# Projections in pairs on 64-row tiles beside the scores, with one pool of seven PSUM banks

## The chip, the core and the metric

The kernel runs on one core of a Trainium2 chip. A core has a matrix engine (TensorE, PE in the profile, with its weight loads shown apart as PEld), a vector engine (DVE), a scalar engine (ACT), a third one for elementwise work (POOL), and a queue (SP) that issues all of this kernel's DMAs. Matmul results go to PSUM, which has eight banks of 128 x 512 floats. DVE and ACT read PSUM; POOL works on the other memory, SBUF. The metric is the device time of one execution in microseconds, lower is better.

## The reference

Two attention blocks, A and B, each over 2048 tokens of 512 features with 32 heads of 16 features. They are computed alike, but A masks its scores to a window of 256 tokens (a query sees itself and the 255 tokens that come before it), and B has no mask. The outputs stand side by side.

```python
B, S, D = x.shape                      # 1, 2048, 512
qkv = (x @ wqkv).reshape(B, S, 3, H, Dh).transpose(2, 0, 3, 1, 4)
q, k, v = qkv[0], qkv[1], qkv[2]
scores = einsum("bhqd,bhkd->bhqk", q, k) * (Dh ** -0.5)
mask = (idx[:, None] - idx[None, :] >= 0) & (idx[:, None] - idx[None, :] < 256)   # block A only
scores = where(mask, scores, -1e9)
p = softmax(scores)
out = einsum("bhqk,bhkd->bhqd", p, v).transpose(0, 2, 1, 3).reshape(B, S, D) @ wo
```

## The kernel before

Heads go in 8 groups of four, queries in 4 chunks of 512, so each block has 32 units (group, chunk). Precise products are made of faster ones: each operand is split into a rounded part and a remainder, and a product is the sum of three matmuls (part by part, part by remainder, remainder by part).

**Projections** (letter `p` in the order; `project_qk`, `project_v`, `products`, L189). One projection makes 128 x 512 results from a contraction over 512 features: 4 slices of 128 features, three matmuls each, so 12 matmuls 128 rows deep and 512 columns wide, into one bank. ACT takes the result out (L254, L331, or L250 for the first pair of heads' groups, where DVE still subtracts from the bank); q and k are split by POOL and written to DRAM, from where they are loaded in the layout that the scores need (tiles `oq` for q, `opk` for k). There are 96 such projections in the first part of the program, 48 for each block.

**Row maxima** (`m` for block A, L427, `e` and `m` for block B, L379, from `max_item` and `max2`). For 128 queries, two heads' scores are made at once: two matmuls 48 rows deep, one on rows 0 to 63 of the array and one on rows 64 to 127, into two adjacent banks. DVE reduces them to maxima (A: a masked copy L436 and a reduction L437; B: one reduction L383).

**The transpose** (`t`, `max_rows`, L505). When a unit's maxima are all there, DVE splits them in three (tile `nm`, 48 columns), PE transposes them by one matmul, ACT copies them out and two small DMAs put them as three further rows under q. So the subtraction of the maximum happens inside the score matmul.

**Scores** (`s`, `scores`, L538). Two heads, again one on each half of the array's rows, 51 rows deep, each into a bank of its own; ACT's exponential (L545) takes them out, POOL zeroes what the mask hides (L555).

**Weighing** (`w` for A at L584, L569 for B). The values are multiplied onto the exponentials of four heads at once, 17 columns each, on four tiles of 32 columns of the array.

So the array is used in four shapes: whole (projections), two tiles of 64 rows (maxima, scores), four tiles of 32 columns (weighing), and 64 columns for the transpose's 48.

The program has two parts. In the first part all of block A's attention, all 96 projections of q, k and v, and the first maxima of block B run in a fixed order, the string `ORDER_A`, one letter a step; `ORDER_P` says which projection each `p` is. The loop at the end takes one letter after the other and issues it on PE, whatever its operands' state: the engines then wait for one another by semaphores. The class `Model` keeps an estimated clock for each engine; from it the loop decides when loads and stores are issued on SP, and when work that follows (the splits on POOL and DVE) is issued, but not the order on PE. In the second part block B's scores and weighing run by another fixed pattern (`ORDER`), with the output projections in between.

In the first part the banks are three kinds: three single ones (`e`) for scores, one (`o`) in which a unit's weighing accumulates, and two pairs (`p`) for maxima. A projection or a transpose takes an `e` bank, or while no scores have begun half of a `p` pair.

## Time and profile before

| | |
|---|---|
| median of 3 runs | 1828.41 us (1828.36 to 1829.36) |
| the profiled execution's own time | 1835.78 us |
| its span | 1834.0 us, of which the first part until the first weighing of block B 558 us |
| TensorE matmuls in the profile | 14392, of which L189 1536, L538 2752, L427 512, L379 2048, L505 64 |

The page of the profile gives for each engine its busy time, and below it the chain of work that ended last. PE is drawn as busy nearly throughout, but matmuls are pipelined and their ends are modelled, so a row's length says little; the distance from one row's start to the next one's is what the work took on PE, with any wait in it. The rows of the timeline merge equal instructions: "x12" are twelve matmuls. The columns are start, length, engine, line, operation, tiles, shape and count.

### The profile page before, as it was taken

How to read it: one execution, taken by the hardware profiler on the slowest of the kernel's cores; microseconds unless marked ns; L12 is line 12 of the kernel's file. 1: busy time of each engine (PE TensorE's matmuls, PEld its weight loads, DVE VectorE, ACT ScalarE, POOL GpSimd, SP SyncE). 2: the span in 40 equal slices, each digit the busy share in tenths (PEclk: the TensorE clock that was granted, in tenths of full speed). 3: DMA queues.
4: the chain of work that ended last, by engine and by line, in shares of the span. 5: the costliest groups of instructions: out<-in, count | busy, mean ns of one | idle time of the engine just before them, and what ended most of it. 6: DMA issues, size and time to landing. Idle time of an engine off the chain costs nothing.

```text
span 1834.0 us, 37708 instructions
## 1 busy us (share of the span) xinstructions
PE 1815.2 (99%) x14392; PEld 902.5 (49%) x14392; DVE 1529.6 (83%) x2275; ACT 1404.5 (77%) x2750; POOL 648.8 (35%) x1333
## 2 busy tenths in 40 slices
PE   8999999999999999999999999999999999999999
PEld 6666656666664444444344444444444444444436
DVE  4677677766779777799999999999999999999901
ACT  4366656565548777799999999999999999999983
POOL 0367877564673333023321023430012322122320
PEclk9999999999999999999999999999999999999999
DMA  8755756545554222311210131121031121010012
GB/s 263 205 176 185 219 174 188 164 157 153 170 180 112 93 78 82 97 29 34 63 37 17 30 67 48 29 63 31 16 75 29 34 63 36 17 49 13 31 36 92
DMA packets 129158, 166.72 MB, mean 91 GB/s; under 512 B 23013, under 2 KB 58853, under 8 KB 128965
## 3 DMA queue, kind: packets, MB, share of 16 engines
q1 hardware_dynamic: 128976, 164.31, 30.4%
q8 instruction: 113, 1.85, 0.4%
q14 instruction: 69, 0.56, 0.1%
HBM read 94.49 MB, written 68.19 MB: 89 GB/s over the span
## 4 chain that ended last, share of the span: by engine, by line
PE 96%; DVE 2%; ACT 1%; DMA 0%; POOL 0%; SPq 0%; issue 0%; ACTq 0%
PE ps_all L569 29%; PE ps_all L189 20%; PE ps_all L538 20%; PE ps_all L379 19%; PE ps_all L584 4%; PE ps_all L427 3%; ACT p L545 1%; DVE mt L437 1%; PE ps_all L505 1%; DVE ps_all L436 0%; DVE mt L383 0%; DMA in<-xT_A 0%; DMA opk<-parts 0%; POOL p L555 0%; POOL x L139 0%
## 5 line engine op out<-in xcount | busy, mean ns | idle before, releaser
L545 ACT ACTIVATE p<-ps_all 128x512 f32<-128x512 f32 x2432 | 1260.8, 597 | 154.9 <-PE ps_all L538 99.9
L383 DVE TENSOR_REDUCE mt<-ps_all 128x2 f32<-128x1024 f32 x1516 | 1194.4, 867 | 72.6 <-PE ps_all L379 72.1
L538 PE MATMUL ps_all<-oq,opk 51*128 51x512 f32 (+2 forms) x2752 | 781.4, 408 | 6.0 <-ACT p L545 5.4
L379 PE MATMUL ps_all<-opk,oq 48*128 48x512 f32 x2016 | 674.3, 438 | 0.3
L569 PE MATMUL ps_all<-p,vt 128*17 128x256 f32 (+1 forms) x6056 | 587.8, 460 | 0.5 <-ACT ou L595 0.5
L538 PEld LDWEIGHTS ps_all<-oq,opk 51*128 51x128 f32 x2752 | 399.0, 185 | 193.4 <-ACT p L545 170.9
L379 PEld LDWEIGHTS ps_all<-opk,oq 48*128 48x128 f32 x2016 | 308.2, 184 | 313.8 <-DVE mt L383 176.8
L555 POOL TENSOR_SCALAR_AFFINE_SELECT p<-p 128x256 f32<-128x256 f32 x480 | 179.8, 407 | 151.6 <-ACT p L545 144.7
L569 PEld LDWEIGHTS ps_all<-p,vt 128*17 128x17 f32 x6056 | 100.7, 95 | 223.8 <-issue 213.1
L189 PE MATMUL ps_all<-x,w 128*128 128x512 f32 x768 | 201.0, 412 | 6.1 <-ACT x L138 5.9
L454 POOL TENSOR_TENSOR mu<-mt 128x16 f32<-128x16 f32 x31 | 6.8, 221 | 503.6 <-DVE mt L383 503.6
L436 DVE COPY_PREDICATED ps_all<-mone,ps_all 128x256 f32<-128x256 uint16 x224 | 94.8, 423 | 93.1 <-PE ps_all L427 92.2
L189 PEld LDWEIGHTS ps_all<-x,w 128*128 128x128 f32 x768 | 144.2, 194 | 48.0 <-ACT x L138 6.9
L437 DVE TENSOR_REDUCE mt<-ps_all 128x2 f32<-128x512 f32 x224 | 155.2, 693 | 7.7
L623 POOL TENSOR_TENSOR rd<-ld,minus 128x32 f32<-128x32 f32 x15 | 81.9, 5458 | 219.2 <-DMA ld<-od 219.2
L254 ACT ACTIVATE raw<-ps_all 128x512 f32<-128x512 f32 x56 | 33.5, 598 | 108.7 <-PE ps_all L189 106.4
L584 PE MATMUL ps_all<-p,vt 128*17 128x384 f32 (+2 forms) x1408 | 96.3, 389 | 0.0
L189 PE MATMUL ps_all<-w_v,x 128*128 128x512 f32 x384 | 95.6, 398 | 0.0
L427 PE MATMUL ps_all<-opk,oq 48*128 48x384 f32 (+2 forms) x512 | 91.5, 378 | 1.9 <-DVE mt L437 1.6
L189 PE MATMUL ps_all<-w_o,x_o 128*128 128x512 f32 x384 | 92.5, 395 | 0.0
L189 PEld LDWEIGHTS ps_all<-w_o,x_o 128*128 128x128 f32 x384 | 70.6, 188 | 29.5 <-issue 13.6
L189 PEld LDWEIGHTS ps_all<-w_v,x 128*128 128x128 f32 x384 | 70.0, 188 | 18.7 <-issue 2.7
(74 smaller groups left out, 742.4 us busy)
## 6 DMA issues: line engine op xcount, KB each, us to landing
parts<-st SPq DMA_DIRECT2D x64, 512.0 KB
oq<-parts SPq DMA_DIRECT2D x128, 128.0 KB
opk<-parts SPq DMA_DIRECT2D x128, 128.0 KB
od<-ou SPq DMA_DIRECT2D x64, 256.0 KB
vd<-vst SPq DMA_DIRECT2D x32, 272.0 KB
oq<-parts SPq DMA_DIRECT2D x128, 64.0 KB
opk<-parts SPq DMA_DIRECT2D x128, 64.0 KB
t<-od SPq DMA_DIRECT2D x32, 256.0 KB
```

Source lines behind the costliest of these rows:

```text
L189: nc.tensor.matmul(ps, l(u), r(v), start=start and k == 0, stop=stop and k == n - 1)
L379: nc.tensor.matmul(ps[:, n], q[rows, 128 * qt:128 * qt + 128], k[rows, kc * QC:kc * QC + QC], start=True, stop=True)
L383: nc.vector.tensor_reduce(out=m[:, a:a + len(heads), r, qt, kc], in_=ps, axis=AX.X, op=ALU.max)
L427: nc.tensor.matmul(two[:, a, 0:w], opq[b, g, c][rows, r, 128 * qt:128 * qt + 128], opk2(g)[rows, r, t0:t1], start=True, stop=True)
L436: nc.vector.copy_predicated(two[:, :, 256:384], later, two[:, :, 0:128])
L437: nc.vector.tensor_reduce(out=m[:, :, r, qt, 0], in_=two[:, :, 128:384], axis=AX.X, op=ALU.max)
L538: nc.tensor.matmul(ps[x][:, col:col + n1], opk2(g)[rows, pr, 128 * k:128 * k + 128], opq[b, g, c][rows, pr, q0:q0 + n1], start=True, stop= ...
L545: nc.scalar.activation(p[:, a0 + x, :w], ps[x][:, :w], AF.Exp, scale=SCALE)
L555: nc.gpsimd.affine_select(out=v, in_=v, pattern=[[0, 2], [sign, 128]], compare_op=ALU.is_ge, fill=zero_fill, base=base, channel_multiplier ...
L569: nc.tensor.matmul(o[32 * j:32 * j + VW, q0:q1], vt[(g // 2) % 2][:, kt, vc:vc + VW], pts[1, g, c, kt, j // 2][:, j % 2, q0:q1], start=kt ...
L584: nc.tensor.matmul(o[32 * j:32 * j + VW, q0:q0 + w], vt[(g // 2) % 2][:, kt, vc:vc + VW], pts[b, g, c, m, j // 2][:, j % 2, col:col + w], ...
L623: nc.gpsimd.tensor_tensor(rd, ld, minus, op=ALU.pow)
```

## The change

**Projections on half tiles.** Forty of the 96 projections run as twenty pairs, each in four steps (letter `g`, `half_rows`, L331 of the changed kernel). The contraction of 128 features of each slice is cut into rows 0 to 63 and rows 64 to 127. In the first two steps the upper half of the array works on rows 0 to 63 of the one projection into the one bank, while the lower half works on rows 64 to 127 of the other projection into another bank; in the last two steps it is the other way round, and each bank accumulates what was missing. One step is 6 times two matmuls 64 rows deep, so a pair of projections is 48 half-height matmuls in 24 twos. So that no bank is written by both halves of the array at once, PE waits before the third step, by an added dependency, for an instruction of another engine that read a result of PE from after the second step. Other letters stand between the second and the third step for that.

**One pool of banks.** The three `e` banks and the two `p` pairs become one pool `u` of seven adjacent banks (`o` moves to bank 0). Maxima take two free neighbours, all else any free ones; of several that would do, the one with the fewest free neighbours is taken.

**The transpose.** `nm` becomes two constant tiles of 2 x 32 columns with the unused columns zero; the transpose becomes two matmuls of 32 columns, which write rows 0 to 31 and 32 to 63 of the bank. The array's shape for it is then the weighing's, 32 columns.

**The order.** `ORDER_P` and `ORDER_A` are written anew: 56 letters `p`, 80 letters `g`, and the same numbers of `m`, `s`, `w`, `t` and `e` as before. The model's constants for a change of the array's shape differ by shape. The second part's order on PE is the same but for the second matmul of each transpose; one projection stands behind the first part's last weighing.

How the order moves on PE. Before, in the late part of block A, a projection of 12 matmuls (L189, operands `x` of the tokens and `w` of the weights) stands between scores (L538) and maxima (L379, L427):

```order
L538 MATMUL ps_all<-oq_6_3_4867,opk_73 128x384 x2
L538 MATMUL ps_all<-oq_6_3_4867,opk_73 128x128 x2
L189 MATMUL ps_all<-w_v_3436,x_2_0_2762 128x512 x3
L189 MATMUL ps_all<-w_v_3620,x_2_1_2848 128x512 x3
L189 MATMUL ps_all<-w_v_3636,x_2_2_2914 128x512 x3
L189 MATMUL ps_all<-w_v_3666,x_2_3_2987 128x512 x3
L379 MATMUL ps_all<-vt_75,qe 128x512 x2
L427 MATMUL ps_all<-opk_74,oq_7_2_5454 128x384 x2
L538 MATMUL ps_all<-oq_7_0_5070,opk_74 128x384 x2
L538 MATMUL ps_all<-oq_7_0_5070,opk_74 128x128 x2
```

Each `p` of this kind goes from tiles of 64 rows to the whole array and back. After, in the same stretch, this is the end of one first step, the work between it and the second step, and the second step's beginning (L331 takes turns between the two projections of a pair, L491 are maxima of A, L603 scores):

```order
L331 MATMUL ps_all<-x_3_1_3382,w_2_0_4288 128x512
L331 MATMUL ps_all<-w_v_3652,x_0_1_2037 128x512
L491 MATMUL ps_all<-opk_76,oq_7_1_5545 128x384 x2
L603 MATMUL ps_all<-oq_6_3_5106,opk_75 128x384 x2
L603 MATMUL ps_all<-oq_6_3_5106,opk_75 128x128 x2
L331 MATMUL ps_all<-x_3_2_3407,w_2_0_4288 128x512
L331 MATMUL ps_all<-w_v_3772,x_0_2_2091 128x512
```

All of it is in one shape, tiles of 64 rows. In the whole first part the array's shape changes 393 times before and 265 times after, and the runs in the whole array are 86 before and 46 after, counted in the two orders.

The transposes stood in a shape of their own between two others, here behind the weighing (L584) and ahead of scores:

```order
L584 MATMUL ps_all<-p_6_3_1_0_5562,vt_76 17x256 x2
L584 MATMUL ps_all<-p_6_3_1_1_5599,vt_76 17x256 x2
L505 LDWEIGHTS nm_7_1_5571
L505 MATMUL ps_all<-ident,nm_7_1_5571 48x128
L538 MATMUL ps_all<-oq_7_0_5070,opk_74 128x384 x2
```

After, they are two matmuls each, next to the weighing in its shape (L649 is the weighing, L570 the transpose):

```order
L491 MATMUL ps_all<-opk_75,oq_4_3_3592 128x384 x2
L570 LDWEIGHTS nm_74
L570 MATMUL ps_all<-ident,nm_74 32x128
L570 LDWEIGHTS nm_74
L570 MATMUL ps_all<-ident,nm_74 32x128
L649 MATMUL ps_all<-p_3_3_2_0_3576,vt_78 17x384 x2
L649 MATMUL ps_all<-p_3_3_2_1_3586,vt_78 17x384 x2
```

The diff, cut to its core:

```diff
+CHUNK = 6
 ORDER_P = (
-    "Aq00 Aq01 Ak00 Av13 Av00 Av03 Aq02 Av20 Ak01 Av10 Av21 Ak02 Av02 Av33 Aq03 Av01 Ak03 Av12 Av11 Aq13 Aq10 "
+    "Aq00 Ak00 Av11 Av10 Aq01 Av03 Ak01 Ak02 Av01 Av13 Aq02 Av12 Av02 Aq03 Av00 Ak03 Av23 Ak11 Av20 Ak10 Av21 "
...
 ORDER_A = (
-    "ppppppppppmmpmmpmmpmmpmmpmmtppmmpmmspsmmptpmsmswsmmpmsmwsmptmmspmswmsmpsmwsmmpmswsmmpmsmwtsmmswsmpmm"
+    "pppppppppmmpmmppmmggmmpmmgtmgmmpmmgsgmspmsgmsgmstwmmmppmsgsmgmmpmsgmmgmtwwmmspmsgsmgmswsgmsgmwtssmws"
...
-        self.mode, self.turn = "f", 170
-        self.banks = {"e": [0] * 3, "p": [0] * 2, "o": [0]}
+        self.mode, self.turn = "f", dict(f=210, h=200, c=139)
+        self.banks = {"u": [0] * 7, "o": [0]}
...
+    def take2(self):
+        self.t["PE"] = max(self.t["PE"], self.pair())
+        free = self.free()
+        n = min((free[i] + free[i + 3], i) for i in range(6) if free[i + 1] and free[i + 2])[1]
+        self.banks["u"][n:n + 2] = [self.NEVER] * 2
+        return n
...
+    nmt = [cst.tile([128, 2, 32], BF16, name=f"nm{i}") for i in range(2)]
...
+    def half_rows(stage, pairs, banks):
+
+        turn, q0 = divmod(CHUNK * stage, 12)
+        for q in range(q0, q0 + CHUNK):
+            k, i = divmod(q, 3)
+            u, v = ((0, 0), (0, 1), (1, 0))[i]
+            for a in range(2):
+                l, r = pairs[a ^ turn][k]
+                rows = slice(64 * a, 64 * a + 64)
+                op = nc.tensor.matmul(view(banks[a ^ turn]), l(u)[rows], r(v)[rows], start=turn == q == 0,
+                                      stop=turn == 1 and q == 11)
+                if turn and q == a == 0:
+                    tc.add_manual_dep(op.ins, min(since)[2].ins.name, LANDED, reason="the row tiles change banks")
+        M.pe("h", CHUNK * 233)
...
-        nc.tensor.transpose(ps[:48, :128], nm.rearrange("p a s j q -> p (a s j q)"), ident)
-        nt = sb.tile([48, 128], F32, name=f"ntr_{n}", tag="ntr")
-        nc.scalar.activation(nt, ps[:48, :128], AF.Copy)
+        for a in range(2):
+            nc.tensor.transpose(ps[32 * a:32 * a + 32, :128], nm[:, a], ident)
+        nt = sb.tile([64, 128], F32, name=f"ntr_{n}", tag="ntr")
+        op = nc.scalar.activation(nt, ps[:64, :128], AF.Copy)
...
-        banks = [M.take("e") for _ in range(heads)]
+        banks = [M.take("e" if b else "u") for _ in range(heads)]
...
+        elif x == "g":
+            if stage == 0:
+                two = its_a[nb:nb + 2]
+                nb += 2
+                banks = [M.take("u") for _ in range(2)]
+            half_rows(stage, [(pairs_qk if f == project_qk else pairs_v)(*a) for f, *a in two], banks)
+            stage += 1
+            if CHUNK * stage == 12:
+                since.clear()
+            elif CHUNK * stage == 24:
+                stage = 0
+                for (f, *a), bank_ in zip(two, banks):
+                    (end_qk if f == project_qk else end_v)(*a, bank_, view(bank_))
+                    made.add((f, *a))
```

`since` collects, from the end of the second step on, each evacuation or reduction that ACT or DVE is given, with the model's time for it; the dependency goes to the one that is done first. `end_qk` and `end_v` are the second halves of `project_qk` and `project_v`, split off unchanged.

More of the change, by code (lines that the diff above doesn't have):

```diff
@@ L201, in view, with take2, release2 @@
         pool, n = bank
-        first, width = {"e": (0, 1), "o": (3, 1), "p": (4, 2), "s": (6, 1)}[pool]
-        n = first + width * n + (pool == "e" and n > 2)
+        if pool == "u":
+            return ps_all[:, n + 1]
+        first, width = {"e": (1, 1), "o": (0, 1), "p": (4, 2), "s": (6, 1)}[pool]
+        n = first + width * n
         return ps_all[:, n] if width == 1 else ps_all[:, n:n + 2]
+    def take2():
+        n = M.take2()
+        return [("u", n), ("u", n + 1)], ps_all[:, n + 1:n + 3]
+    def release2(banks, t):
+        for b in banks:
+            M.release(b, t)
     ident = cst.tile([128, 128], BF16, name="ident")
@@ L422, in max_item @@
         w = t1 - t0
-        bank = M.take("p")
-        two = view(bank)
+        banks, two = take2()
         for a in range(2):
@@ L929, in load_next @@
         f(*a)
+    stage, two, banks = 0, None, None
     todo_a = list(ORDER_A)
```

138 lines of the change are left out of this document (81 added, 57 removed), and 6 rows, old and new, of the table ORDER_P.

## The prediction

> **What bounds the kernel now.** I read the page first: its engines, then its chain of work.
>
> ```profile
> PE 1815.2 (99%) x14392; PEld 902.5 (49%) x14392; DVE 1529.6 (83%) x2275; ACT 1404.5 (77%) x2750; POOL 648.8 (35%) x1333
> ...
> PE 96%; DVE 2%; ACT 1%; DMA 0%; POOL 0%; SPq 0%; issue 0%; ACTq 0%
> ```
>
> The chain runs on PE for 96% of the span, so what PE needs for an instruction is what counts. The change touches the first part, so next come the sums by stretch, the first part and the rest (columns: length, then busy time of PE, PEld, DVE, ACT, POOL, the granted clock, the DMA engines' share, GB/s), and two stretches of 7 us in it:
>
> ```profile
> 5.00:558.00 553.00, 543.91 (x3924) 357.73 (x3924) 379.93 (x798) 309.50 (x612) 328.70 (x630) 0.99 0.60 187
> 558.00:1834.00 1276.00, 1271.25 (x10470) 544.78 (x10469) 1148.49 (x1476) 1093.04 (x2137) 316.64 (x688) 1.00 0.18 49
> 262.00:269.00 7.00, 6.97 (x20) 4.98 (x20) 3.41 (x12) 2.25 (x5) 2.42 (x7) 0.52 0.59 200
> 276.00:283.00 7.00, 7.00 (x31) 4.97 (x24) 4.71 (x10) 3.34 (x7) 5.17 (x10) 0.52 0.36 121
> ```
>
> In the first part DVE is busy for 69%, ACT 56%, POOL 59%: PE is ahead of them all, and none would stop it from being some per cent shorter. In two stretches the granted clock was 0.52; they cost this execution 2 x 7 x 0.48 = 6.7 us. It took 1835.78 us where the median is 1828.41, 7.4 us less, so I suppose that the timed runs are without them. The terms below are differences on PE, worked out from rows at full clock, and I take them off the median.
>
> What does PE lose in a change of the array's shape? The timeline of PE, a projection (L189) between scores and maxima on 64-row tiles, twice:
>
> ```profile
> 472.07 0.50 PE L538 MATMUL ps_all<-oq,opk 51*128 51x384 f32 x4
> 472.50 3.02 PE L189 MATMUL ps_all<-w_v,x 128*128 128x512 f32 x12
> 475.45 0.50 PE L379 MATMUL ps_all<-vt,qe 48*128 48x512 f32 x2
> 475.78 0.34 PE L427 MATMUL ps_all<-opk,oq 48*128 48x384 f32 x2
> 475.96 0.40 PE L538 MATMUL ps_all<-oq,opk 51*128 51x384 f32 x4
> 476.28 3.02 PE L189 MATMUL ps_all<-x,w 128*128 128x512 f32 x12
> 479.23 0.44 PE L427 MATMUL ps_all<-opk,oq 48*128 48x384 f32 x2
> 479.51 0.40 PE L538 MATMUL ps_all<-oq,opk 51*128 51x384 f32 x4
> 479.75 0.39 PE L427 MATMUL ps_all<-opk,oq 48*128 48x384 f32 x2
> ```
>
> and, from the start of the program, projections that follow each other:
>
> ```profile
> 26.42 2.88 PE L189 MATMUL ps_all<-x,w 128*128 128x512 f32 x12
> 29.14 2.88 PE L189 MATMUL ps_all<-w_v,x 128*128 128x512 f32 x12
> 31.86 2.88 PE L189 MATMUL ps_all<-x,w 128*128 128x512 f32 x12
> ```
>
> Starts count, not lengths. Among its like a projection takes 2.72 us (227 ns a matmul); alone 2.95 (472.50 to 475.45), 0.23 more. Ahead of it, the scores of a 384 and a 128 wide two take 0.24 where the next is in the same shape (479.51 to 479.75), 0.32 where a projection follows (475.96 to 476.28): 0.08 more. And the first two in the shape after it take 0.28 at a width of 384 (479.23 to 479.51) where the second takes 0.18 (475.78 to 475.96): 0.10 more. So one projection alone costs 0.40 us beyond its work: two changes of shape at some 0.09 each, and in either shape a first instruction whose successor comes 0.10 late.
>
> **The change part by part.** *What half-height twos cost.* Block B's scores and maxima are twos of the same width, 512, on the two halves, with 51 and 48 rows instead of 64:
>
> ```profile
> 901.25 0.50 PE L538 MATMUL ps_all<-oq,opk 51*128 51x512 f32 x1
> 901.25 0.73 PE L379 MATMUL ps_all<-opk,oq 48*128 48x512 f32 x2
> 901.59 0.62 PE L538 MATMUL ps_all<-oq,opk 51*128 51x512 f32 x2
> 901.82 0.40 PE L379 MATMUL ps_all<-opk,oq 48*128 48x512 f32 x1
> 902.20 1.05 PE L569 MATMUL ps_all<-p,vt 128*17 128x512 f32 x8
> ...
> L379 PEld LDWEIGHTS ps_all<-opk,oq 48*128 48x128 f32 x2016 | 308.2, 184 | 313.8 <-DVE mt L383 176.8 <-issue 131.5 <-ACT p L545 3.0
> ```
>
> Three twos: the second begins 0.34 us after the first (the late second once more), the third 0.23 after the second. In the timeline's starts over all of block B the second interval is 0.228 to 0.238. These twos wait for banks, those of a projection stand in sixes with nothing to wait for; I take 0.232, and 0.228 and 0.238 as ends. 480 twos take the place of 480 whole matmuls at 0.227: +2.4 us, +0.5 to +5.3.
>
> The Trainium skill, TensorE: Matmul & The Clock Gate, section The mechanism, has a rule that speaks against this: a weight load overlaps with running matmuls only where the row group differs. Here each half's next weights go to the half that is at work. By that rule loads and matmuls would take turns; the time is among the rivals. The trace does not agree: 0.23 us from the second two to the third has no room for a load of 0.18 behind a matmul.
>
> *Shapes saved by projections.* There are 40 runs in the whole array fewer, and all but one of the 79 runs of `g` stand between maxima or scores. 40 x 0.40 = -16.0 us. To the edges of these rows, 0.38 to 0.42, it is -15.2 to -16.8.
>
> *Shapes saved by transposes.* What one costs now:
>
> ```profile
> 394.25 0.45 PE L538 MATMUL ps_all<-oq,opk 51*128 51x128 f32 x4
> 394.54 0.34 PE L427 MATMUL ps_all<-opk,oq 48*128 48x384 f32 x2
> 394.81 1.06 PE L584 MATMUL ps_all<-p,vt 128*17 128x256 f32 x16
> 395.79 0.24 PE L505 MATMUL ps_all<-ident,nm 128*48 128x128 bf16 x1
> 395.96 0.55 PE L538 MATMUL ps_all<-oq,opk 51*128 51x128 f32 x4
> ...
> 368.20 0.62 PE L584 MATMUL ps_all<-p,vt 128*17 128x256 f32 x8
> 368.75 0.44 PE L427 MATMUL ps_all<-opk,oq 48*128 48x384 f32 x2
> ```
>
> 16 weighing matmuls ahead of a transpose take 0.98 us, 8 ahead of maxima 0.55, so 8 alone 0.43 and the change 0.12, the same in front of a transpose as of anything. The transpose takes 0.17 with the change behind it, so some 0.06 itself. Of the 128 changes of shape that go in the first part, 80 are the projections'; the other 48 at 0.10 are -4.8 us, and 11 further late seconds on 64-row tiles at 0.10 are -1.1. The second matmul of 33 transposes costs 0.06 each, +2.0 us (no row has a second one: it could be nothing, or 0.17 as a lone one, 0 to +5.6). In block B 31 transposes stand behind a weighing: 31 x (0.06 - 0.11) = -1.6 (-3.4 to +1.9). Together -5.5, between -9.3 and +1.6.
>
> *Steps entered.* A 384 wide two that follows a short one takes 0.23 instead of 0.18 (394.25 to 394.54 is 0.29 for 0.06 + 0.23), its successor's weights being late. 45 of the 79 runs of `g` come behind a 384 wide two: at most 45 x 0.05 = +2.2, or 0 where it would have been so anyway.
>
> *Waits.* These are waits in the first part (in all, times, longest), the first one of the weight loads:
>
> ```profile
> PEld ps_all L538 <- ACT p L545: 28.6, 63, 0.9
> ...
> PE ps_all L538 <- ACT p L545: 5.2, 13, 0.7
> ...
> PE ps_all L427 <- DVE mt L437: 1.6, 6, 0.6
> ...
> PE ps_all L538 <- DMA oq<-ntr: 0.3, 1, 0.3
> ```
>
> Most come from scores whose bank ACT hasn't emptied. I walked both orders with the prices above and looked, at each wait of PE for ACT or DVE in the first part, how far back stands the matmul which that engine reads. Nearer than 1.0 us are 69 before, and these lose 17 us in the trace, all the others 7. After, 62 are nearer. So I expect the same losses, though a pair keeps two of seven banks for 6.5 to 13 us. The new wait ahead of the third step has 1.9 us or more of other work in front of it in all 20 pairs, and in two alone PE still names it, 1.3 and 1.4 us behind: nothing. What is queued behind it would be the third step and the maxima after it, and DVE and ACT would run dry. What is lost where the same work of the others stands in a part that is 3% shorter I put at +2 us, with 0 and +20 as ends: from none of the waits to one more microsecond in each pair.
>
> ACT, DVE and SP have the same instructions (a copy of 64 partitions for one of 48 has the same width); POOL has one memset more at the start. The first pair of projections waits for the second weights instead of the second tokens, while the third then waits less: nothing.
>
> The sum: 2.4 - 16.0 - 5.5 + 2.2 + 2 = -14.9 us; 1828.4 - 14.9 = **1813.5 us**.
>
> **The rivals.** *Banks run out* (slower). With five banks left for maxima in neighbours and for scores, PE stands before L491 and L603 in the middle of each pair. The sum without waits is -16.9, so from 0.85 us a pair on the gain is gone; at 1.1 us it is 1828.4 - 16.9 + 22 = 1833.5. For it speaks that PEld waits 63 times for ACT now; against it the count of near waits, 62 for 69.
>
> *Others set the pace* (same). Chains through DRAM (projection, store, load, maxima, transpose, scores) fix the first part's length, and PE waits for what it saved: 1828. Against it, PE waited once for a DMA of these chains, 0.3 us, and DVE, ACT and POOL have a third of their time left.
>
> *Weights take turns with matmuls* (slower). A two costs 0.184 + 0.227 = 0.41 us, 480 x 0.18 = +86 us on the forecast: 1900. Only the rows' 48 and 51 instead of 64 leave room for it.
>
> *The shapes stay.* The runs of `g` would drain PE like a shape of their own: 79 runs x 0.4 instead of 40: 1828.4 - 14.9 + 32 = 1845. They have the tile size of maxima and scores, and L379 and L538 change places without loss at 901.59.
>
> **How the numbers follow.** The forecast holds with 0.79, of these 0.06 with less than half of the gain. Banks have 0.10, the same pace 0.06, weights 0.03, shapes 0.02. The range: the ends of the prices alone, -16.8 - 9.3 + 0.5 + 0 = -25.6 and -15.2 + 1.6 + 5.3 + 2.2 = -6.1, would all have to fall to one side; I take 1806 below. Above I reach to 1829, past the rival that ends at 1828; the slower ones, 0.15, lie beyond. A measurement of this kernel tells 0.2% (3.7 us) from no change: faster 0.79, same 0.06, slower 0.15.
>
> **What would show it.** In the changed profile's timeline: six twos of L331 that start 0.23 us apart, the next row behind the sixth at most 0.24 later; weighing rows that pass to L570 without the 0.12; the second part beginning at some 545 us instead of 558, with 1274 us behind it. A stretch at half clock more or less moves the profile by 3.4 us and is no part of this (without both, 538). I would be wrong if the waits of PE or PEld for L491, L603 or L331 grow by over 10 us, or if twos of L331 stand 0.3 us apart or more.

## The result and the profile after

The changed kernel takes 1828.90 us (median of 22 runs, 1825.90 to 1835.41); the kernel before, run beside it, 1829.77 us (22 runs, 1828.36 to 1833.00). The ratio is 0.9996, with a 95% interval of 0.9990 to 1.0003: no difference that this measurement can tell, where 14.9 us less was forecast.

The page of the changed kernel, its engines and its chain of work:

```profile
PE 1800.0 (98%) x14936; PEld 910.1 (50%) x14936; DVE 1530.1 (84%) x2275; ACT 1399.9 (77%) x2750; POOL 651.3 (36%) x1334
...
PE 91%; DVE 5%; ACT 1%; DMA 1%; issue 1%; SPq 0%; POOL 0%; ACTq 0%; DVEq 0%; POOLq 0%
```

PE is busy for 15 us less, as meant (both traces hold stretches at half clock, in which a matmul lasts longer: 13.7 us of them before, 17.1 after, the last microseconds left out). But the chain, which ran on PE for 96% of the span, now runs on it for 91%: DVE has 5%, ACT, DMA and issue 1% each. So what PE saved it partly stands and waits. The sums of the two parts (the first weighing of block B, L634, is now at 548.84 us) and two stretches at their boundary, in the columns of the prediction:

```profile
5.00:549.00 544.00, 526.07 (x4441) 364.84 (x4445) 381.05 (x799) 305.70 (x614) 330.53 (x630) 0.99 0.62 190
549.00:1826.00 1277.00, 1273.94 (x10499) 545.29 (x10491) 1147.88 (x1475) 1092.25 (x2136) 317.42 (x688) 1.00 0.18 49
...
544.48:547.90 3.42, 2.83 (x15) 1.43 (x13) 3.14 (x5) 2.91 (x6) 1.77 (x2) 1.00 0.85 206
547.90:558.14 10.24, 10.24 (x51) 3.06 (x50) 6.92 (x10) 5.87 (x12) 0.05 (x1) 0.50 0.87 150
```

The first part has 9 us less, 558.27 to 548.84. In the first row PE is idle for 17.9 us where it was for 9.1 (553.00 - 543.91). The last row is new: just behind the boundary the granted clock was 0.50 for 10.24 us.

The first part's waits, by what ended them, PE's own and then those of its weight loads (in all, times, longest):

```profile
PE ps_all L491 <- DVE mt L501: 4.1, 9, 0.7
PE ps_all L603 <- ACT p L610: 2.9, 6, 0.7
PE ps_all L491 <- ACT p L610: 2.3, 7, 0.8
PE ps_all L208 <- DVE st L297: 1.4, 2, 1.0
PE ps_all L603 <- DVE mt L501: 1.3, 3, 0.6
PE ps_all L491 <- DMA oq<-parts: 1.1, 2, 0.7
PE ps_all L491 <- ACT raw L291: 0.5, 1, 0.5
...
PE ps_all L331 <- ACT p L610: 0.2, 1, 0.2
...
PEld ps_all L491 <- ACT p L610: 12.5, 30, 1.0
PEld ps_all L491 <- DVE mt L501: 12.3, 24, 1.0
PEld ps_all L603 <- ACT p L610: 11.9, 27, 0.9
```

Before, scores (L538, now L603) did most of the waiting, for ACT, 28.6 us of weight loads; that is 11.9 now. Instead the row maxima wait (L427, now L491). PE stood in front of them for 1.6 us and now does for 4.1 + 2.3 + 1.1 + 0.5 = 8.0. For ACT's exponentials (L610), which they were never seen to wait for before, their weight loads wait 12.5 us; and DVE's L501 keeps them 12.3 us, where the kernel before has these rows, 15.9 us together:

```profile
PEld ps_all L427 <- DVE ps_all L436: 8.2, 18, 0.6
PEld ps_all L427 <- DVE mt L437: 7.7, 21, 0.8
```

So the maxima's weight loads don't wait longer for DVE than before; new are their waits for ACT, and 4.5 us in which those of scores wait for L501. Between 135 and 296 us no projection runs on half tiles (L331 has no row there), and these are PE's own waits in that stretch:

```profile
PE ps_all L491 <- DVE mt L501: 2.7, 6, 0.7
PE ps_all L491 <- ACT p L610: 1.9, 5, 0.8
PE ps_all L603 <- ACT p L610: 1.8, 4, 0.7
PE ps_all L603 <- DVE mt L501: 0.7, 2, 0.5
```

They are 7.1 us of the 10.6 that the same four rows have in the whole first part. Between 296 and 524 us, where 15 of the 20 pairs stand, the same four come to 2.6.

How a pair holds its banks, in PE's timeline of one pair's first step and of the end of its last one:

```profile
356.34 0.43 PE L491 MATMUL ps_all<-opk,oq 48*128 48x384 f32 x2
356.57 0.39 PE L331 MATMUL ps_all<-x,w 64*128 64x512 f32 x1
356.61 0.39 PE L331 MATMUL ps_all<-w_v,x 64*128 64x512 f32 x1
356.80 0.39 PE L331 MATMUL ps_all<-x,w 64*128 64x512 f32 x1
...
357.73 0.39 PE L331 MATMUL ps_all<-x,w 64*128 64x512 f32 x1
357.77 0.39 PE L331 MATMUL ps_all<-w_v,x 64*128 64x512 f32 x1
357.96 0.38 PE L491 MATMUL ps_all<-opk,oq 48*128 48x384 f32 x2
...
364.52 0.39 PE L331 MATMUL ps_all<-x,w 64*128 64x512 f32 x1
364.68 0.40 PE L491 MATMUL ps_all<-opk,oq 48*128 48x384 f32 x2
365.60 0.46 PE L491 MATMUL ps_all<-opk,oq 48*128 48x384 f32 x2 [0.51 <-ACT raw L291]
```

and ACT's, which takes the two results out:

```profile
364.95 0.60 ACT L291 ACTIVATE raw<-ps_all 128x512 f32<-128x512 f32 x1 [1.92 <-PE ps_all L331]
365.44 0.59 ACT L396 ACTIVATE vst<-ps_all 128x512 f32<-128x512 f32 x1
```

The step itself is as forecast: six twos 0.23 us apart, and the next row behind the sixth (357.73 to 357.96) 0.23 later. But the pair took its banks at 356.57 and gave them back at 365.55 and 366.03. The maxima at 365.60 stand until the first of them is read out. Such waits, for a bank that a pair itself held, are rare: 0.9 us in the whole first part, by the count that follows.

I counted banks in both traces, from a bank's first matmul to the end of its last reader, between 50 and 530 us. A whole projection holds its bank for 3.8 us (mean), one on half tiles for 10.8 (8.5 to 16.7). Of seven banks 4.0 are busy on average before and 4.7 after, and two free neighbours, as maxima need them, are missing for 30% of that time before and for 50% after. I also laid the trace's starts beside the prediction's walk through the program with its prices, and counted as a wait each start more than 0.08 us later than priced. Leaving the half-clock stretches out, the waits that end with the freeing of a bank are 21.4 us before and 32.4 after in the first part; those of maxima among them went from 4.6 to 17.4, those of scores fell. This count, the time, and the granted clock are the measures below.

Which bank each matmul writes and each reader reads follows from the program, so each such wait can be put to the bank's user before. Counted against short intervals of the same kind in the traces (their 15th percentile) in place of the prices, the waits are 22.8 us before and 33.1 after. In the changed kernel 13.0 of them are maxima waiting for a bank that scores used last, or scores for one that maxima used. Before, where each kind had banks of its own, there are none of these. The waits of maxima for maxima and of scores for scores fell from 20.8 to 16.5. And they don't lie where the pairs hold their banks: 6.3 us fall in the 222 us in which a pair holds two banks, 17.5 between 135 and 296 us, where no pair stands (12.3 and 15.0 in two traces of the kernel before). While a pair holds its banks 5.1 of seven are busy on average and two free neighbours are missing for 63% of the time, else 4.3 and 40%. So the pool is tighter with a pair in it, but the waits come elsewhere.

### The profile page after: what moved, and what is told of

Same layout as the page of the kernel before. It is cut to its first block, busy times and chain, and to the rows that moved or that the text cites. A ratio compares the mean times of both kernels' runs of the same rounds, so it can differ in the third digit from the quotient of the medians.

```text
span 1828.5 us, 38989 instructions
## 1 busy us (share of the span) xinstructions
PE 1800.0 (98%) x14936; PEld 910.1 (50%) x14936; DVE 1530.1 (84%) x2275; ACT 1399.9 (77%) x2750; POOL 651.3 (36%) x1334
## 4 chain that ended last, share of the span: by engine, by line
PE 91%; DVE 5%; ACT 1%; DMA 1%; issue 1%; SPq 0%; POOL 0%; ACTq 0%; DVEq 0%; POOLq 0%
PE ps_all L634 29%; PE ps_all L444 19%; PE ps_all L603 18%; PE ps_all L208 12%; PE ps_all L331 5%; PE ps_all L649 4%; PE ps_all L491 3%; DVE mt L501 2%; ACT p L610 1%; DVE mt L448 1%; DVE ps_all L500 1%; DMA in<-xT_A 1%; PE ps_all L570 0%; DVE nm L553 0%; DMA oq<-parts 0%
## 5 line engine op out<-in xcount | busy, mean ns | idle before, releaser
L610 ACT ACTIVATE p<-ps_all 128x512 f32<-128x512 f32 x2432 | 1257.6, 597 | 187.0 <-PE ps_all L603 122.5
L603 PE MATMUL ps_all<-oq,opk 51*128 51x512 f32 (+2 forms) x2752 | 773.2, 406 | 4.9 <-ACT p L610 3.1
L634 PE MATMUL ps_all<-p,vt 128*17 128x256 f32 (+1 forms) x6056 | 590.0, 462 | 0.5 <-ACT ou L660 0.5
L603 PEld LDWEIGHTS ps_all<-oq,opk 51*128 51x128 f32 x2752 | 397.8, 185 | 181.6 <-ACT p L610 155.2
L634 PEld LDWEIGHTS ps_all<-p,vt 128*17 128x17 f32 x6056 | 100.7, 95 | 224.1 <-issue 213.5
L501 DVE TENSOR_REDUCE mt<-ps_all 128x2 f32<-128x512 f32 x224 | 155.2, 693 | 7.7
L208 PE MATMUL ps_all<-x,w 128*128 128x512 f32 x468 | 121.7, 410 | 6.3 <-ACT x L157 6.3
L331 PE MATMUL ps_all<-x,w 64*128 64x512 f32 x600 | 124.7, 391 | 0.2 <-ACT p L610 0.2
L491 PE MATMUL ps_all<-opk,oq 48*128 48x384 f32 (+2 forms) x512 | 97.2, 375 | 8.9 <-DVE mt L501 4.1
L208 PEld LDWEIGHTS ps_all<-x,w 128*128 128x128 f32 x468 | 87.4, 194 | 32.5 <-ACT x L157 7.0
L649 PE MATMUL ps_all<-p,vt 128*17 128x384 f32 (+2 forms) x1408 | 95.9, 389 | 0.4 <-DMA vt<-vd 0.2
L331 PE MATMUL ps_all<-w_v,x 64*128 64x512 f32 x360 | 92.9, 391 | 0.0
L331 PEld LDWEIGHTS ps_all<-x,w 64*128 64x128 f32 x600 | 88.8, 185 | 7.2 <-ACT p L610 0.6
```

Source lines behind the costliest of these rows:

```text
L208: nc.tensor.matmul(ps, l(u), r(v), start=start and k == 0, stop=stop and k == n - 1)
L331: op = nc.tensor.matmul(view(banks[a ^ turn]), l(u)[rows], r(v)[rows], start=turn == q == 0, stop=turn == 1 and q == 11)
L491: nc.tensor.matmul(two[:, a, 0:w], opq[b, g, c][rows, r, 128 * qt:128 * qt + 128], opk2(g)[rows, r, t0:t1], start=True, stop=True)
L501: op = nc.vector.tensor_reduce(out=m[:, :, r, qt, 0], in_=two[:, :, 128:384], axis=AX.X, op=ALU.max)
L603: nc.tensor.matmul(ps[x][:, col:col + n1], opk2(g)[rows, pr, 128 * k:128 * k + 128], opq[b, g, c][rows, pr, q0:q0 + n1], start=True, stop= ...
L610: op = nc.scalar.activation(p[:, a0 + x, :w], ps[x][:, :w], AF.Exp, scale=SCALE)
```

## The experiments

All times are medians; ratios are to the kernel before on the same chip, with 95% intervals. "Priced" is the first part's work on PE by the prediction's prices, "banks" the waits for a bank and "busy" the mean number of busy banks just described, "clock" the median of the mean granted clocks of the timed runs.

| kernel | us | ratio | priced | banks, us | busy | clock |
|---|---|---|---|---|---|---|
| before | 1829.77 | | 506.9 | 21.4 | 4.0 | 0.999 |
| after | 1828.90 | 0.9996 (0.9990 to 1.0003) | 489.7 | 32.4 | 4.7 | 0.996 |
| same | 1829.77 | 0.9994 (0.9985 to 1.0003) | 506.9 | 22.7 | 4.0 | 1.000 |
| t_only | 1830.96 | 0.9996 (0.9987 to 1.0005) | 507.2 | 23.7 | 4.1 | 0.999 |
| old_order | 1838.13 | 1.0032 (1.0020 to 1.0045) | 507.2 | 28.5 | 4.0 | 0.999 |
| whole | 1865.68 | 1.0192 (1.0175 to 1.0208) | 502.4 | 48.5 | 4.0 | 0.996 |
| short | 1826.32 | 0.9977 (0.9964 to 0.9989) | 489.7 | 26.9 | 3.7 | 0.995 |
| before_short | 1828.24 | 0.9987 (0.9979 to 0.9996) | 506.9 | 20.3 | 3.0 | 0.999 |
| lru | 1839.80 | 1.0049 (1.0033 to 1.0066) | 489.7 | 43.7 | 4.7 | 0.997 |
| fill32 | 1829.02 | 0.9992 (0.9978 to 1.0006) | 491.5 | 32.2 | 4.7 | 0.997 |
| old_six | 1915.03 | 1.0462 (1.0447 to 1.0476) | 507.2 | 94.1 | 3.5 of 6 | 0.995 |
| start | 1830.08 | 1.0001 (0.9991 to 1.0011) | 489.7 | 32.0 | 4.7 | 0.995 |
| unmasked | 1825.91 | 0.9974 (0.9963 to 0.9985) | 491.5 | 25.4 | 4.1 | 0.996 |

### The kernel before, once more

> The kernel before as it is, for the granted clock of its undisturbed executions, which is known of the profiled one alone (0.996, two stretches at half clock). Theory W (the prices on PE hold, and the saved time went into new waits for PSUM banks and into stretches at half clock): clock 0.996 to 0.998, as the changed kernel's runs (0.991 to 0.999), spread over 3 us. Rival C (the gain is there and half-clock stretches, which only the changed kernel has, take it away): clock 0.999 in nearly every execution, spread under 2 us. Time by both 1829.8 us, the median of 22.

No edit. 1829.77 us; its profile has no half-clock stretch before the last microseconds, a span of 1827.7 us and the first weighing of block B at 551.8 us. So the execution shown before the change was an unusual one, and 551.8 is what the changed kernel's 548.84 is to be compared with. The clock of the runs is 1.000, as rival C had it and not theory W; the spread of 5.5 us is wider than either expected.

### The transposes alone

> The kernel before with the transposes alone changed: two matmuls of 32 columns from constant tiles. The order stays, so few transposes stand next to a weighing in the first part: 18 changes of shape fewer, at my prices nothing there and -1.4 us in block B. Theory W: 1828.4 to 1829. Rival O (other engines and the chains through DRAM set the first part's pace, PE's savings there are absorbed): the same -1.4. The prediction's -5.5 for the transposes as such, without the new order: 1824.3.

```
-        nc.tensor.transpose(ps[:48, :128], nm.rearrange("p a s j q -> p (a s j q)"), ident)
+        for a in range(2):
+            nc.tensor.transpose(ps[32 * a:32 * a + 32, :128], nm[:, a], ident)
```

1830.96 us, 0.9996 (0.9987 to 1.0005). In the order of before few transposes stand beside a weighing: the walk finds 18 changes of shape fewer in the first part, which the second matmuls pay back (507.2 priced for 506.9). By itself this part is worth nothing that can be measured; the 1824.3 of a full -5.5 is out.

### The pool and the transposes, with the order of before

> The changed kernel with both order strings of the kernel before, so no projections in pairs: against the one with the transposes alone only the pool of seven banks and the model's constants differ, the order on PE is the same. Waits of PE nearer than 1.0 us behind the work they need: 76, with the transposes alone 68. Theory W: maxima now wait for banks that ACT empties, some 2 to 8 us slower, 1831 to 1837. If the pool as such costs nothing: 1828.7.

```
 ORDER_P = (
-    "Aq00 Ak00 Av11 Av10 Aq01 Av03 Ak01 Ak02 Av01 Av13 Aq02 Av12 Av02 Aq03 Av00 Ak03 Av23 Ak11 Av20 Ak10 Av21 "
+    "Aq00 Aq01 Ak00 Av13 Av00 Av03 Aq02 Av20 Ak01 Av10 Av21 Ak02 Av02 Av33 Aq03 Av01 Ak03 Av12 Av11 Aq13 Aq10 "
...
```

This is t_only with one pool of seven, since PE's instructions and their order are the same in both; the model's constants differ too, and with them the times at which loads, stores and splits are issued. It takes 1838.13 us, 7 us more, and a little over the 1831 to 1837 that were expected. PE's waits in its first part:

```profile
PE ps_all L603 <- ACT p L610: 5.2, 14, 0.6
PE ps_all L491 <- DVE mt L501: 3.1, 6, 1.2
PE ps_all L603 <- DVE mt L448: 1.1, 1, 1.1
PE ps_all L603 <- DVE mt L501: 1.0, 2, 0.6
```

Scores now stand for DVE's reading of maxima, which in the kernel before could not happen, since maxima had their own banks. So even without one projection on half tiles, sharing the banks in this order costs 7 us, 4.8 of which are waits for banks; 5.7 us are maxima and scores standing behind each other. Where the rest lies is not settled; the clock is nearly the same (a straight line through the runs, time against clock, gives at 1.000 for t_only 1829.0, for this one 1835.3).

### The new order with whole projections

> The changed kernel with its own order, but each pair's first step makes the whole first projection on the whole array and its third step the whole second one; the second and fourth steps do nothing. So only the half tiles are undone. At my prices PE has 12.7 us more work (350 changes of shape for 271 up to the first weighing of block B), and 110 near waits for 62. Theory W: 1841 or more, up to 1850 with the waits. Rival O: as the changed kernel, 1829 within 3 us, since what PE needs for a projection does not matter. Rival C: 1841.

```
-            half_rows(stage, [(pairs_qk if f == project_qk else pairs_v)(*a) for f, *a in two], banks)
-            stage += 1
...
+            if stage in (0, 2):
+                f, *a = two[stage // 2]
+                one, ps1 = room()
+                for _ in products(ps1, (pairs_qk if f == project_qk else pairs_v)(*a)):
+                    pass
...
+            stage = (stage + 1) % 4
```

1865.68 us, 36.8 more than with half tiles, where the changes of shape account for 12.7 (502.4 - 489.7); it is also 16 us above the 1850 that was expected at most. Waits for banks are 48.5 us, though no more banks are busy than before the change; the profile has 28 us at half clock in the first part. So the half tiles are worth at least what they were priced at, in this order. And the order is fitted to its work: 1.4 us pieces replaced by 2.9 us ones at every second letter `g` bring 16 us of waits. That limits what an experiment that moves work on PE can show, so those that follow leave PE's order alone.

### Shorter holding by maxima, in both kernels

> The changed kernel with the DVE's reading of the first block's row maxima cut to the last 128 columns, without the mask: about 0.75 us less for each of 288 pairs of banks; the instructions of TensorE and their order are as in the changed kernel. It leaves out the mask and the older blocks of those maxima. Worked out from its trace, the half-height projections hold a bank for 10.5 us where whole ones hold it for 3.8, the mean number of busy banks between 50 and 530 us is 4.7 of 7 against 4.0 before, and no two free neighbours are there for 50% of that time against 30%. Theory H (the pairs hold banks so long that others wait for them): busy banks fall to about 4.1, the waits for banks from 32 us to 20 or less, time 1814 to 1820. Rival O (the new order itself brings consumers near to producers, whatever the banks): within 3 us of the changed kernel, or as much faster as the kernel before becomes by the same edit.

> The kernel before with the same cut of the DVE's reading of row maxima (the mask and the older blocks of those maxima are left out). Here maxima have banks of their own, and 21 us go in waits for banks, 4.6 of them ahead of maxima. Theory H: it gains less than the changed kernel does, 3 to 6 us, 1824 to 1827. Rival O: the same gain in both kernels. If DVE is a pace-setter of its own in both, both gain over 10 us.

The edit is the same in both (here in the changed kernel):

```
         if i < 2:
-            for a in range(2):
-                op = nc.vector.tensor_tensor_reduce(junk[:, :w], two[:, a, 0:w], wmask[:, 256 - w:], 1.0, -3.0e38,
-                                               ALU.add, ALU.max, accum_out=m[:, a, r, qt, 0:1])
...
-            nc.vector.copy_predicated(two[:, :, 256:384], later, two[:, :, 0:128])
-            op = nc.vector.tensor_reduce(out=m[:, :, r, qt, 0], in_=two[:, :, 128:384], axis=AX.X, op=ALU.max)
+        op = nc.vector.tensor_reduce(out=m[:, :, r, qt, 0], in_=two[:, :, w - 128:w], axis=AX.X, op=ALU.max)
```

By the medians the expectation of theory H failed: 1826.32 us where 1814 to 1820 was expected. Against the kernel before that is 0.9977 where the changed kernel has 0.9996, some 3.5 us; the kernel before gains 2.4 us by the same edit (0.9987), less than the 3 to 6 of theory H and near to what rival O expects. Fewer banks are busy than theory H had (3.7 for 4.1), but the waits for banks are 26.9 us and not 20. The traces and the clocks add this. The first parts, of the kernel before with the edit, and then of the changed kernel with it (which ends 5 us earlier) and two stretches in it:

```profile
5.00:549.00 544.00, 534.49 (x3924) 353.32 (x3924) 218.18 (x478) 308.97 (x612) 328.54 (x630) 1.00 0.63 190
```

```profile
5.00:544.00 539.00, 523.59 (x4435) 364.29 (x4435) 219.79 (x478) 304.00 (x612) 329.21 (x630) 0.99 0.64 191
...
312.50:315.90 3.40, 1.90 (x14) 1.44 (x16) 0.43 (x1) 0.03 (x1) 0.87 (x4) 1.00 1.01 302
315.90:319.30 3.40, 3.40 (x16) 2.71 (x13) 0.68 (x2) 1.60 (x3) 3.31 (x7) 0.51 1.06 385
```

In the first of the two stretches PE is busy for 1.90 of 3.40 us, mostly since maxima wait for a load of q (1.6 us at the longest), and in the second the clock is 0.51. DVE is busy for 160 us less in both kernels. With half of each half-clock stretch taken off, block B's first weighing comes at 539.4 us in the changed kernel with the edit, 5.5 earlier than without it (544.9), and at 549.0 in the kernel before, 2.6 earlier (551.4 to 551.8). But most of the waits for banks stay (26.9 us of 32.4): maxima no longer wait for DVE, and more often for ACT (13.5 us, 9.8 without the edit). And the runs' clock is lower still, 0.995, while the kernel before stays at 0.999. A straight line through each kernel's runs, time against clock, gives at a clock of 1.000: before 1829.5 (31 runs), changed 1825.0 (22), short 1817.5 (12), before_short 1827.1 (12). So at like clock the edit is worth 7.4 us in the changed kernel and 2.5 in the one before. These are extrapolations, since short never ran above 0.997. At that clock it took 1820.4 and 1822.9 us, and the changed kernel 1826.8 to 1829.6.

### Another choice among the free banks

> The changed kernel, in which the pool hands out the bank (or the two neighbours) that has been free longest by the planner's clock, instead of the one with the fewest free neighbours. Rival C (the choice of a bank just freed makes any error of the planner's clock a wait): waits for banks fall by 10 us or more, 1819 or less. Theory H (too few banks are free to choose among: one or none is free besides in 25 of the 32 us of such waits): within 5 us of the changed kernel, rather slower, since free neighbours are split up; by the program 76 weighted steps stand under 1 us behind what they wait for, against 62.

```
-            n = min((free[i] + free[i + 2], i) for i in range(7) if free[i + 1])[1]
+            n = min((self.banks["u"][i], i) for i in range(7) if free[i + 1])[1]
...
-        n = min((free[i] + free[i + 3], i) for i in range(6) if free[i + 1] and free[i + 2])[1]
+        n = min((max(self.banks["u"][i:i + 2]), i) for i in range(6) if free[i + 1] and free[i + 2])[1]
```

1839.80 us, 11 more than the changed kernel, and the waits for banks 43.7 us, not less. The choice of the changed kernel, which keeps free neighbours together, is not what costs it its gain; rival C falls. Theory H's "within 5 us of the changed kernel" failed as well.

### More filler at the boundary

> The changed kernel with 32 filler multiplications instead of 16 where the second part's maxima begin, 1.9 us more of work in all. In the changed kernel's trace the clock is halved for 10.2 us from 547.9 us on, just behind this place, which costs some 5 us; the mean granted clock of its timed runs is mostly 0.997, where that of the kernel before is 1.000. Theory K (that stretch follows from too little work of TensorE around 545 us and is there in most of the runs): the stretch goes, the clock of the runs is 0.999 or more, time 1825 to 1827. Rival: the stretch stays or moves, time 1829 to 1832.

```
-FILL = 16
+FILL = 32
```

1829.02 us. In its profile the place has full clock:

```profile
546.80:550.20 3.40, 2.89 (x18) 1.01 (x16) 3.40 (x5) 3.40 (x8) 1.28 (x1) 1.00 1.08 147
550.20:553.60 3.40, 3.40 (x34) 1.53 (x30) 3.40 (x6) 2.77 (x6) 0.00 (x0) 1.00 1.11 176
```

But the timed runs have a clock of 0.997, hardly more than the 0.996 before, and the two stretches of 3.4 us in the first part, at 257 and 284 us, are in this profile too. So theory K explains one stretch in one trace and no gain; the time is that of its rival. One of the 12 runs had a clock of 1.000 and took 1822.65 us, with 1.9 us of filler in it: that is what the changed kernel takes without half-clock stretches, some 1821 to 1825 with the line above.

### One bank fewer

> The kernel with the one pool and the transposes in 32 columns but the order of before (no half-height projections), with six banks in the pool instead of seven; TensorE's instructions and their order are the same as with seven, which ran in 1838.1 us with 4.0 banks busy on average and 25 us of waits for banks. It prices a bank in this order: the half-height projections keep 0.7 of a bank more than whole ones did. Theory H (banks are scarce, each that is held longer brings waits): 15 us or more over the run with seven, 1853 or more, or 10 us and more for 0.7 of a bank. Rival O (the order's near neighbours bring the waits, and a bank more or less is no matter): 1838 to 1845.

```
-        self.banks = {"u": [0] * 7, "o": [0]}
+        self.banks = {"u": [0] * 6, "o": [0]}
```

1915.03 us, 76.9 more than with seven banks and the same instructions of PE in the same order; the waits for banks are 94.1 us for 28.5. PE's waits in the first part:

```profile
PE ps_all L491 <- ACT p L610: 12.5, 23, 1.0
PE ps_all L208 <- ACT p L610: 12.4, 20, 1.3
...
PE ps_all L603 <- ACT p L610: 5.0, 13, 0.9
PE ps_all L208 <- DVE mt L501: 4.5, 10, 1.1
PE ps_all L491 <- DVE mt L501: 4.0, 8, 0.9
```

So banks are scarce: with 4.0 of 7 busy on average one bank less costs 4% of the time. I take it as an upper bound for what 0.7 of a bank costs in the changed kernel, since the new order was made with pairs in it and this one was not made for six banks; no run shows that cost itself. Rival O's 1838 to 1845 is out.

### The first projections

> The changed kernel with its first projections in the order Aq00 Aq01 Ak00 Av11 Av10, the second one again by the weights that are there first, as in the kernel before. In the changed kernel's trace the stretch up to 50 us loses 2.4 us more in waits than in the trace of before. If that is this order: 2 to 3 us faster, 1826 to 1827; if the first loads set the end of that stretch anyway: 1829.

```
-    "Aq00 Ak00 Av11 Av10 Aq01 Av03 Ak01 Ak02 Av01 Av13 Aq02 Av12 Av02 Aq03 Av00 Ak03 Av23 Ak11 Av20 Ak10 Av21 "
+    "Aq00 Aq01 Ak00 Av11 Av10 Av03 Ak01 Ak02 Av01 Av13 Aq02 Av12 Av02 Aq03 Av00 Ak03 Av23 Ak11 Av20 Ak10 Av21 "
```

1830.08 us, no gain. The first 50 us lose as much as they did; the wait only went elsewhere. PE's waits up to 50 us, in this kernel:

```profile
PE ps_all L208 <- ACT x L157: 6.4, 1, 6.4
PE ps_all L491 <- DMA opk<-parts: 2.9, 2, 2.6
```

The projections no longer wait for DVE (1.4 us in the changed kernel), but with Ak00 later the first maxima wait 2.9 us for the load of its keys.

### A version put together from this

> A version put together from what the runs showed: the changed kernel with row maxima of the first block read in one instruction over the last 256 columns and without the mask (a softmax may subtract any number that is near the row's maximum, so the mask of the maxima is left out and the oldest 128 columns of three; the probabilities are still masked), first projections in the order Aq00 Aq01 Ak00, and 32 filler multiplications at the start of the second part. Theory H: the banks of maxima are held about 0.45 us less, two thirds of the gain of the shortest reading; with the 2.4 us of the start and the boundary's stretch 1820 to 1825. Rival: the half-clock stretches eat it, 1826 to 1829.

```
-                op = nc.vector.tensor_tensor_reduce(junk[:, :w], two[:, a, 0:w], wmask[:, 256 - w:], 1.0, -3.0e38,
...
-            nc.vector.copy_predicated(two[:, :, 256:384], later, two[:, :, 0:128])
-            op = nc.vector.tensor_reduce(out=m[:, :, r, qt, 0], in_=two[:, :, 128:384], axis=AX.X, op=ALU.max)
+        op = nc.vector.tensor_reduce(out=m[:, :, r, qt, 0], in_=two[:, :, max(w - 256, 0):w], axis=AX.X, op=ALU.max)
```

and the edits of fill32 and start. 1825.91 us, 0.9974 (0.9963 to 0.9985): 0.26% faster than the kernel before, and faster than the changed kernel with its 0.9996 (0.9990 to 1.0003). It lies between the two expected ranges and decides neither. The waits for banks are 25.4 us, and the clock of its runs is 0.996, so here too the clock keeps a part of the gain. Since fill32 and start by themselves gave nothing, I put the gain down to the shorter reading of maxima, which the kernel before can have as well in a smaller measure (before_short, 0.9987).

## Why the prediction was wrong

**Twos on half tiles: right.** +2.4 us were put for 0.232 a two. The intervals within a step of L331 have medians of 0.227 to 0.234, and a whole step takes 1.387 us (median) for 1.392, as in the rows shown. The rival "weights take turns" is out.

**Shapes and steps entered: right.** 16.0 and the first part's share of 5.5 were to go and 2.2 to come. The same walk, over the changed program, prices the first part at 489.7 us for 506.9, 17.2 less; entering a step costs no more than was put (beyond the prices all 20 first and 20 third twos lose 0.6 and 0.0 us, so the added wait ahead of the third step is free, too). The second part, with half of the half-clock stretches taken off, has 1274.7 us behind the first weighing where 1274 was put; before it has 1275.7. That microsecond isn't sure: start has the same second part, and its trace has 1276.6 us there at full clock. "The shapes stay" is out. Had there been no wait more, block B would have begun 17 us earlier than before; it began 6.5 to 6.9 earlier.

**Waits: this is the step that failed.** "So I expect the same losses", and +2 us. The first part's losses beyond the prices, without half-clock stretches' half, are 49.5 us for 38.7 to 39.6 before: 10 us more. The waits for banks alone grew by 11.0, and the first 50 us, put at nothing, lose 2.4 more, while others shrank a little. The first weighing came, at like clock, at 544.9 us instead of the 538 of the forecast. They are waits for banks, as in the rival "banks run out", which had 0.10 and 0.85 us a pair as the point from which the gain is gone; but not by the mechanism that it named, PE standing in the middle of each pair. Within the 190 us from the first to the last step of all pairs only 7 us are lost beyond the prices; the other 46, half clock included, lie outside. What is new there are the 13.0 us in which maxima and scores stand behind each other in the same banks. By the prediction's own sign, waits for L491, L603 or L331 up by over 10 us, the kinds part: PE's own ahead of L491 grew by 6.4 us and those of its weight loads by some 11, those of L603's weight loads fell by some 12. The argument against that rival was a count: 62 near waits for 69. It counted how far back the work stands, and took all near waits as alike. In the kernel before, maxima waited for DVE alone, and little; in the pool they stand behind ACT as well. That the three `e` banks and the two `p` pairs become one pool had no term in the sum at all, though the program tells beforehand which bank each matmul takes and who used it last.

How sure is this? The waits for banks and who is waited for are in the traces. That sharing the banks costs by itself is shown (old_order, +7 us), and that banks are scarce in the order of before (old_six, +77). That the long holding by the pairs brings the waits is not shown, and the trace speaks against it: 6.3 us in the 222 us in which a pair holds banks, 26.8 in all the rest. In short it isn't the pairs that hold banks for less time but the maxima, so it can't show it either: at like clock the pool gains more by it (7.4 us against 2.5), by the medians not clearly (3.5 against 2.4). An experiment in which the pairs alone give their banks back earlier, and PE's order stays, could not be made: their steps are the order. Open is also why maxima and scores stand behind each other for 13.0 us in the new order and for 5.7 in the old one with the same pool. The new order may by itself bring them nearer to each other, as rival O of the expectations has it; it was not run with separate banks.

**"I suppose that the timed runs are without" half-clock stretches: true before, false after.** The mean clock of the timed runs is 0.999 to 1.000 before and 0.996 after, 0.991 at the least. The prediction carried this over to the changed kernel without a word. 0.0035 of 1829 us are 6.4 us; the line through the changed kernel's runs gives 4.0 (1828.9 - 1825.0). In the profiles each stretch follows 3.4 us in which PE was idle for a part, 4% at the least; the kernel before has these rows, to be set beside those at 544.48 above:

```profile
258.80:262.20 3.40, 2.67 (x28) 1.52 (x26) 2.47 (x5) 2.86 (x8) 3.37 (x9) 1.00 0.36 123
262.20:265.60 3.40, 3.40 (x13) 2.56 (x14) 3.05 (x11) 2.05 (x4) 2.02 (x6) 0.50 0.87 306
```

Cut in 3.41 us pieces on that grid, from 50 us on, the traces have 4 pieces with PE busy for less than 85% before, and 13 after, 9 in short, 15 in lru, 18 in whole, but also 5 in unmasked and 50 in old_six, whose clocks are 0.996 and 0.995, and again 4 in same, which has no stretch before its last microseconds. Not each brings a stretch: of the 13 after, 11 bring none, and in the trace of fill32 two pieces at 164 and 171 us, at 78% and 71%, bring none. So the number of such pieces doesn't tell the clock, and what does is open. The Trainium skill, TensorE: Matmul & The Clock Gate, section A second HAM failure mode: psum-queue depth-cycling, tells of a kernel in which PE's short pauses while PSUM banks go round set the clock back and forth. The rows here agree in part: ahead of the stretches of these two kernels the pauses are waits of at most 0.7 us for banks, and the clock is halved for 3.4 to 10.2 us behind them, but most pieces of that kind bring nothing. Other causes do as well: in short (312 us) and start (37 us) a stretch follows a wait of 1.6 and 2.6 us for a load. That the shared pool's waits are what lowers the clock of the runs is therefore likely here, and not shown.

**The sum.** 17.2 us less in the first part and 1.0 in the second, 10 us of waits back: 8.2 us less at full clock, 1821.6 us, which the run of fill32 at clock 1.000, without its filler (1820.8), and the line through the changed kernel's runs (1825.0) bracket within 4 us. The clock takes 4 to 6 us of that. The rest, one to three microseconds, isn't accounted for. "Others set the pace", which gave 1828, has the number by luck and not the mechanism: PE waits for loads of the chains through DRAM 1.5 us in all, and in the first part DVE has 30% of its time left and ACT 44%. That the time lies just inside the stated range says as little: the range was drawn up to 1829 to take in that rival, and the gain of 14.9 us isn't there.

## What to carry to other kernels

Price a change of PE's work by rows as here, but ask of PSUM as well who will stand behind whom in a shared pool that had banks of its own; a count of near waits doesn't see it. When a theory says where the waits come from, look whether they lie there: here the pairs held the banks, and the waits were elsewhere. Where PE is the bound and nearly never idle, ask what each new pause does to the granted clock, and compare kernels at like clock before saying that an edit did nothing. An order fitted to its pieces is itself a resource: moving work in it (whole) costs more than the work.

## What was not expected of the hardware

- PE's clock falls to 0.50 for 3.4, 6.8 or 10.2 us after 3.4 us in which it was idle for only 10 to 22% of the time in the traces of the two kernels, in pauses of at most 0.7 us (2.83 us busy of 3.42 at 544.48); but after 2.89 of 3.40 in fill32 it did not.
- Two half-height matmuls on the two halves of the array, each two with new weights for the same halves, start 0.227 to 0.234 us after the last two (medians of the five intervals within a step, over 80 steps): as fast as one whole matmul of the same work (0.227), though a weight load of 0.185 us (L331) goes to a half that is at work.
